# One spectral-mixing kernel: weight runs of 16 KB with real and imaginary rows interleaved on the partitions, pinned TensorE slots from mode 10 on, and filler matmuls behind modes 44 to 59

## The chip, the cores and the metric

The kernel runs on one core of one Trainium2 chip. The metric is the device time of a run in microseconds (us). Repeated runs are given as a median with the lowest and highest. A ratio below is the mean time of one kernel's fast runs over the mean time of the other's fast runs of the same rounds, so it is not quite the ratio of the medians quoted beside it; it comes with a 95% interval, and a difference under 2% counts as "same".

## The reference, cut to what matters

```python
def _attn_ref(q, k, v):                       # all (8, 8, 576, 64) f32
    phi = lambda x: np.where(x > 0, x, np.exp(x) - 1.0) + 1.0
    q_p, k_p = phi(q), phi(k)
    kv = np.einsum('bhsd,bhse->bhde', k_p, v)
    z = np.sum(k_p, axis=2)
    num = np.einsum('bhsd,bhde->bhse', q_p, kv)
    den = np.einsum('bhsd,bhd->bhs', q_p, z)[..., None] + 1e-06
    return num / den

def _moe_ref(x, w_r, w_i, w_ch):              # x (8, 576, 512); w_r, w_i (64, 512, 512) f32
    X = np.fft.rfft(x, axis=1)                # 64 modes are kept
    Yr = np.einsum('bmd,mde->bme', Xr, w_r) - np.einsum('bmd,mde->bme', Xi, w_i)
    Yi = np.einsum('bmd,mde->bme', Xr, w_i) + np.einsum('bmd,mde->bme', Xi, w_r)
    ...
    y = np.fft.irfft(Y, n=S, axis=1)
    u = x + y
    return u + np.maximum(u @ w_ch, 0.0)
```

The two weight tensors are 2 x 64 x 512 x 512 x 4 B = 134 MB of f32. They are read once, and the transfer casts them to bf16 on the way into on-chip memory (SBUF). Each of the 64 modes needs 2.097 MB of f32, its wr and its wi.

Of the kernel before, what the change touches and what calls it, by code (L numbers as in the profile page):

```python
# [42 lines left out]
def kernel(  # L43
# [18 lines left out]
    XDC = 3 * B * NM  # L62
    XTW = NDC * XDC + 2 * B * NM
# [21 lines left out]

    xt_c = xpool.tile([128, XTW], BF16, name="xt_c")
    nc.vector.memset(xt_c[:, NDC * XDC : XTW], 0.0)
    xt_v = xt_c[:, 0 : NDC * XDC].rearrange("p (c t b m) -> p c t b m", c=NDC, t=3, b=B)

    def xt_cols(dc: int, t: int, kk: int):  # L90

        c0 = dc * XDC + t * B * NM + kk
        return xt_c[:, c0 : c0 + 31 * NM + 1 : NM]
# [3 lines left out]
    q_tile = lambda name: xpool.tile([128, QW], F16, tag="qTE", bufs=B + 1, name=name)  # L97
# [3 lines left out]
    W_KEEP = 8  # L101

    def w_load(kk: int, half: int, pool, tag: str, bufs: int):
        name, src = (("wr", moe_w_r), ("wi", moe_w_i))[half]
        w = pool.tile([128, NDC, D], BF16, tag=tag, bufs=bufs, name=f"{name}{kk}")
        rows_of = src[kk].rearrange("(p dc) e -> p dc e", dc=NDC)
        for dcs in (slice(0, 3), slice(3, 4)) if (kk, half) == (NM - 1, 1) else (slice(0, NDC),):
            tc.keep_in_program_order(nc.gpsimd.dma_start(out=w[:, dcs], in_=rows_of[:, dcs, :]))  # L108
        return w

    w_in: dict[int, list] = {}


    W_PRE = 12
# [4 lines left out]
    n_pre, n_keep = W_PRE // 2, W_KEEP // 2  # L119
# [7 lines left out]
    def w_next():  # L127
        kk, half = pending.pop(0)
        pool, tag, bufs = (wpool, "w", W_KEEP) if kk < n_keep else (wpre, "wp", W_PRE)
        w_in.setdefault(kk, []).append(w_load(kk, half, pool, tag, bufs))  # L130
# [153 lines left out]

    def transform(b, dc):
# [17 lines left out]
        if dc == NDC - 1:  # L303
            pin(nc.vector.tensor_copy(out=xt_v[:, :, 1:3, b, :], in_=xf))
            pin(nc.scalar.mul(out=xt_v[:, :, 0, b, :], in_=xf[:, :, 1, :], mul=-1.0))
# [7 lines left out]
    for b in range(B):  # L313
# [12 lines left out]
        for jj in range(NJJ + 1):  # L326
            form_x(b, jj)
            if b > 0 and jj in (2, 3):
                transform(b - 1, jj - 2)
# [3 lines left out]
    for dc in range(NDC):  # L333
        transform(B - 1, dc)


    def w_get(kk: int):
        if kk not in w_in:
            w_in[kk] = [w_load(kk, half, wpool, "w", W_KEEP) for half in range(2)]
# [7 lines left out]
    FILL = {61: (2, 2, 1), 62: (5, 3, 3), 63: (6,)}  # L347

    def mode_product(kk: int, ps, stage, yt_ps):

        wr, wi = w_get(kk)
        st = stage.tile([128, D], F16, tag="ystage", bufs=2, name=f"ys{kk}")
        fixed = pin if kk >= NF else (lambda ins: ins)
        fill = FILL.get(kk, (0, 0, 0))
        P = ps.tile([128, D], F32, tag="P", bufs=2, name=f"P{kk}")
        for t, w in ((1, wr), (0, wi)):
            for dc in range(NDC):
                fixed(
                    nc.tensor.matmul(  # L359
                        P[dc * 32 : dc * 32 + 32, :], xt_cols(dc, t, kk), w[:, dc, :],  # L360
                        start=(t == 1), stop=(t == 0), tile_position=(0, dc * 32),
                    )
                )
            if t == 1:
                work_slot(kk, 0)
                keep_warm(fill[0])
        if kk % 2 == 0:
            fixed(nc.vector.tensor_copy(out=st, in_=P))  # L368
        else:
            fixed(nc.scalar.copy(out=st, in_=P))  # L370
        work_slot(kk, 1)
        keep_warm(fill[1])
# [6 lines left out]
        keep_warm(fill[2])  # L379

    work: list = []
# [7 lines left out]
    def last_mode(ps):  # L389

        kk = NM - 1
        wr, wi = w_get(kk)
        y_last = ps.tile([128, NDC, 2 * B], F32, tag="P", bufs=2, name="y_last")

        def product(t, w, dcs):
            for dc in dcs:
                c0 = dc * XDC + t * B * NM + kk
                x = xt_c[:, c0 : c0 + (2 * B - 1) * NM + 1 : NM]
                for ec in range(NDC):
                    pin(  # L400
                        nc.tensor.matmul(
# [473 lines left out]
```

## The kernel before: the parts that the change touches

The kernel first forms the attention for 8 batches and their spectra `xt_c`. Then it goes through 64 modes. A mode multiplies the spectra by wr and wi (tile `P`, "the P matmuls"), copies `P` out and turns it (`yt`). Other TensorE work is put between: attention rows in modes 10 to 31 (`nw`), inverse transforms and channel products in modes 32 to 55, and the rows of the last modes (`z`, `yp`, `yb`, `zb`) in modes 56 to 60. After the last mode come a tail of matmuls, adds and the stores.

```python
    xt_c = xpool.tile([128, XTW], BF16, name="xt_c")   # per column: -imag, real, imag
    W_KEEP = 8                                         # 8 half-mode tiles = 4 modes

    def w_load(kk, half, pool, tag, bufs):             # 128 partitions, one 8 KB f32 run each
        name, src = (("wr", moe_w_r), ("wi", moe_w_i))[half]
        w = pool.tile([128, NDC, D], BF16, tag=tag, bufs=bufs, name=f"{name}{kk}")
        rows_of = src[kk].rearrange("(p dc) e -> p dc e", dc=NDC)          # NDC = 4
        for dcs in (slice(0, 3), slice(3, 4)) if (kk, half) == (NM - 1, 1) else (slice(0, NDC),):
            tc.keep_in_program_order(nc.gpsimd.dma_start(out=w[:, dcs], in_=rows_of[:, dcs, :]))
        return w
    # ... cut
    FILL = {61: (2, 2, 1), 62: (5, 3, 3), 63: (6,)}    # filler matmuls

    def mode_product(kk, ps, stage, yt_ps):
        wr, wi = w_get(kk)
        fixed = pin if kk >= NF else (lambda ins: ins) # NF = 32: earlier modes are left to the scheduler
        P = ps.tile([128, D], F32, tag="P", bufs=2, name=f"P{kk}")
        for t, w in ((1, wr), (0, wi)):                # 4 matmuls with wr, then 4 with wi
            for dc in range(NDC):
                fixed(nc.tensor.matmul(
                    P[dc * 32 : dc * 32 + 32, :], xt_cols(dc, t, kk), w[:, dc, :],
                    start=(t == 1), stop=(t == 0), tile_position=(0, dc * 32)))
            if t == 1:
                work_slot(kk, 0)                       # other TensorE work between wr and wi
                keep_warm(fill[0])
        # ... cut: copy P out
        work_slot(kk, 1)
        # ... cut: yt
    # ... cut
    QUADS = (5, 6)                                     # batches stored in one piece of four tiles
    for kk in range(n_early, NM):                      # n_early = 10
        mode(kk)
        if kk < NF:                                    # attention rows, left to the scheduler
            for i in spread(len(tiles), kk - n_early, NF - n_early):
                attention_rows(tiles[i])
```

## Time and profile before

| | before |
|---|---|
| time, first 3 runs | 427.85 us (427.78 to 427.94) |
| span of the profiled run | 425.4 us |
| last weight lands, tail after it | 393.03 us, 32.4 us |
| one mode in the weight stream | 4.916 us |
| DMA share and landed rate, 160 to 180 us | 1.06, 213 GB/s |

The first lines are from the page of before, the part that cuts the span into 40 slices. Each digit of PEclk is the TensorE clock that was granted, in tenths of full speed; each digit of DMA is the busy share of the 16 transfer engines in tenths, 9 being 90% or more. GB/s is what landed, so bf16 for the weights.

```profile
PEclk9999866565555855555555587989999899999998
DMA  9999999999999999999999999999999999998797
GB/s 215 208 208 209 209 210 209 212 212 215 218 211 214 214 212 215 214 213 214 212 214 213 213 214 213 214 214 213 213 213 214 214 213 213 213 213 157 250 394 295
DMA packets 35502, 93.12 MB, mean 219 GB/s; under 512 B 3024, under 2 KB 15696, under 8 KB 35216
```

The DMA row has no gap until slice 36 (383 to 393 us), and the rate is flat. Nearly all packets land in less than 8 KB: one weight packet is 4 KB of bf16.

The second view is the chain of waits of before in order of time: start, length, and what was waited for.

```profile
156.94 18.65 DMA wi<-in_moe_w_i_dram
...
176.60 18.65 DMA wi<-in_moe_w_i_dram
...
196.26 18.65 DMA wi<-in_moe_w_i_dram
...
215.92 18.65 DMA wi<-in_moe_w_i_dram
...
235.59 18.64 DMA wi<-in_moe_w_i_dram
...
378.55 14.44 DMA wi<-in_moe_w_i_dram
393.03 0.30 PE y_last L401 x4
```

Each step of 19.66 us is four modes: a load is issued when the tile of four modes earlier comes free. So a mode takes (235.59 - 156.94) / 16 = 4.916 us. The last line is the first work that the last weight allowed.

The third view is the windows of before: a stretch, its length, the busy time of each engine with its instructions, the granted clock, the DMA share and the landed GB/s.

```profile
core 0: us, PE busy (x) PEld busy (x) DVE busy (x) ACT busy (x) POOL busy (x), PEclk, DMA share, GB/s
12.00:16.00 4.00, 1.11 (x22) 1.22 (x24) 2.80 (x4) 0.62 (x1) 1.30 (x2) 1.00 1.21 207
...
160.00:180.00 20.00, 12.11 (x142) 7.24 (x142) 10.84 (x37) 1.17 (x2) 4.23 (x8) 0.50 1.06 213
...
400.00:405.00 5.00, 5.00 (x34) 1.53 (x32) 4.87 (x5) 4.28 (x8) 0.00 (x0) 1.00 0.99 394
```

The first row is q, k and v, in runs of 2,304 B; the second is weights alone; the third is the store. In all three the transfers are full, so the kernel is bound by them nearly from end to end.

### The profile page before, as it was taken

What the parts mean: (1) busy time and instruction counts of PE and PEld (TensorE: products, weight loads), DVE (VectorE), ACT (ScalarE), POOL (GpSimd) and SP (SyncE); (2) the same over time, 40 slices, a digit from 0 to 9 for tenths busy, and PEclk for the clock granted to TensorE, in tenths of its full rate; (3) what the DMA queues carried; (4) which work ended last, traced back from release to release, by engine and by line L of the source; (5) the groups of instructions that cost most, each with busy time, mean ns of one, the idle gap of its engine ahead of it and who ended that gap; (6) DMA issues with size and microseconds to landing.
All of it is one profiled execution on the core that took longest, in us unless ns stands there. A gap on an engine that the chain in (4) does not pass through costs nothing.

```text
span 425.4 us, 6619 instructions
## 1 busy us (share of the span) xinstructions
PE 285.7 (67%) x2692; PEld 160.0 (38%) x2692; DVE 214.5 (50%) x440; ACT 154.1 (36%) x241; POOL 88.3 (21%) x159
## 2 busy tenths in 40 slices
PE   1358777887119765666333689778677778998992
PEld 0246555674003433333111334434334334473420
DVE  4598999956002755556200433433444244421793
ACT  4677776630102100000000244434443354430781
POOL 4222223222201322122112122112122121110000
PEclk9999866565555855555555587989999899999998
DMA  9999999999999999999999999999999999998797
GB/s 215 208 208 209 209 210 209 212 212 215 218 211 214 214 212 215 214 213 214 212 214 213 213 214 213 214 214 213 213 213 214 214 213 213 213 213 157 250 394 295
DMA packets 35502, 93.12 MB, mean 219 GB/s; under 512 B 3024, under 2 KB 15696, under 8 KB 35216
## 3 DMA queue, kind: packets, MB, share of 16 engines
q0 software_dynamic: 31360, 81.48, 98.3%
q1 hardware_dynamic: 4112, 11.22, 7.1%
q8 instruction: 21, 0.34, 0.3%
q14 instruction: 9, 0.07, 0.0%
HBM read 163.93 MB, written 9.44 MB: 407 GB/s over the span
## 4 chain that ended last, share of the span: by engine, by line
DMA 69%; PE 12%; issue 8%; DVE 7%; ACT 2%; POOL 1%; DVEq 0%; POOLq 0%; ACTq 0%
DMA wi<-in_moe_w_i_dram 51%; DMA wr<-in_moe_w_r_dram 9%; DMA k<-in_k_dram 9%; PE acc L641 3%; PE P L359 2%; DVE x L277 2%; PE acc L680 2%; ACT ke L190 1%; PE z L604 1%; DVE ke L203 1%; DVE k L197 1%; PE zb L631 1%; PE zb L630 1%; DVE qe L203 1%; PE yb L626 1%
## 5 line engine op out<-in xcount | busy, mean ns | idle before, releaser
L359 PE MATMUL P<-wi,xt_c 128*32 128x512 bf16 x252 | 37.9, 536 | 38.7 <-DMA wi<-in_moe_w_i_dram 38.6
L370 ACT CAST ys<-P 128x512 f16<-128x512 f32 x31 | 18.2, 586 | 121.6 <-PE P L359 106.8
L108 POOL DMA_DIRECT2D wr<-in_moe_w_r_dram x64 | 34.1, 533 | 130.6 <-PE P L359 91.0
L368 DVE CAST ys<-P 128x512 f16<-128x512 f32 x32 | 22.1, 691 | 72.0 <-PE P L359 49.8
L108 POOL DMA_DIRECT2D wi<-in_moe_w_i_dram x65 | 34.6, 532 | 111.8 <-PE P L359 88.2
L359 PEld LDWEIGHTS <-xt_c 128*32 128x32 bf16 x504 | 28.7, 156 | 75.8 <-issue 64.4
L359 PE MATMUL P<-wr,xt_c 128*32 128x512 bf16 x252 | 37.6, 550 | 24.6 <-DMA wr<-in_moe_w_r_dram 22.5
L563 DVE TENSOR_TENSOR x_main<-ya,x_main 128x512 f32<-128x512 f32 x32 | 22.1, 691 | 43.7 <-PE ya L559 43.6
L582 PE MATMUL eps<-wch,xTw 128*128 128x512 f16 x144 | 41.2, 414 | 0.0
L144 PEld LDWEIGHTS <-qT 64*128 64x128 f16 (+1 forms) x640 | 25.3, 126 | 41.6 <-issue 21.3
L565 ACT CAST x16w<-x_main 128x512 f16<-128x512 f32 x32 | 19.8, 618 | 37.4 <-DVE x_main L563 37.4
L375 PE MATMUL yt<-pick_sb,ys 128*128 128x16 f16 x252 | 16.6, 176 | 24.1 <-DMA pick_sb<-row_pick 15.2
L590 ACT CAST E<-eps 128x512 f16<-128x512 f32 (+1 forms) x40 | 21.3, 543 | 25.5 <-PE eps L582 25.5
L144 PE MATMUL num<-kv,qT 64*128 64x65 f16 (+1 forms) x320 | 13.8, 227 | 20.7 <-ACT kv L250 18.0
L375 PEld LDWEIGHTS <-ys 128*128 128x128 f16 x252 | 12.3, 103 | 39.8 <-issue 16.6
L190 ACT ACTIVATE qe<-q 128x1152 f16<-128x1152 f16 (+1 forms) x16 | 17.8, 1157 | 17.8 <-DMA q<-in_q_dram 17.8
L219 PE MATMUL qTp<-id,qe 128*128 128x128 f16 x144 | 16.7, 309 | 10.1 <-DVE qe L203 9.5
L144 PE MATMUL nw<-kv,qT 64*128 64x65 f16 (+1 forms) x320 | 22.1, 236 | 1.6 <-DVE x_tail L533 1.0
L277 DVE TENSOR_TENSOR x<-num,rd 128x512 f16<-128x512 f32 x32 | 22.1, 692 | 1.1
L190 ACT ACTIVATE ke<-k 128x1152 f16<-128x1152 f16 x16 | 17.7, 1155 | 6.6 <-DMA k<-in_k_dram 6.0
L690 ACT ACTIVATE acc<-acc 128x512 f32<-128x512 f32 x34 | 18.1, 581 | 2.3 <-PE acc L641 1.3
L219 PEld LDWEIGHTS <-qe 128*128 128x128 f16 x144 | 14.5, 146 | 11.2 <-DVE qe L203 9.9
(104 smaller groups left out, 442.5 us busy)
## 6 DMA issues: line engine op xcount, KB each, us to landing
wr<-in_moe_w_r_dram POOLq DMA_DIRECT2D x64, 512.0 KB, 18.6
wi<-in_moe_w_i_dram POOLq DMA_DIRECT2D x63, 512.0 KB, 18.7
k<-in_k_dram POOLq DMA_DIRECT2D x8, 576.0 KB, 14.5
v<-in_v_dram POOLq DMA_DIRECT2D x8, 576.0 KB, 16.6
out_dram<-x_main SPq DMA_DIRECT2D x9, 512.0 KB, 3.1
q<-in_q_dram POOLq DMA_DIRECT2D x7, 576.0 KB, 13.8
out_dram<-x_main SPq DMA_DIRECT2D x2, 1024.0 KB, 5.2
out_dram<-x_main SPq DMA_DIRECT2D x6, 256.0 KB, 3.4
```

The lines of the kernel that those rows point to most:

```text
L108: tc.keep_in_program_order(nc.gpsimd.dma_start(out=w[:, dcs], in_=rows_of[:, dcs, :]))
L144: mm = nc.tensor.matmul(num[hpo][orow, c0 : c0 + 65], qT[rows, hpp, h2, cols], kv_sb[rows, hpp, h2, :])
L190: pin(nc.scalar.activation(out=ev[:, c], in_=heads(nm, b, c), func=AF.Exp))
L219: nc.tensor.transpose(qT_ps[:, j].rearrange("p t r -> p (t r)"), phi["q", b][:, hpp, j].rearrange("p o d -> p (o d)"), id16,)
L277: nc.vector.tensor_tensor(out=dst.rearrange("p (o c d) -> p o c d", o=2, c=4), in0=nv[:, :, :, 0:64], in1=rden.unsqueeze(3).broadcast_to([ ...
L359: nc.tensor.matmul(P[dc * 32 : dc * 32 + 32, :], xt_cols(dc, t, kk), w[:, dc, :], start=(t == 1), stop=(t == 0), tile_position=(0, dc * 32),)
L368: fixed(nc.vector.tensor_copy(out=st, in_=P))
L375: nc.tensor.matmul(yt_ps[:, ec, kk % 8, :], st[:, ec * 128 : ec * 128 + 128], pick_sb)
L563: pin(nc.vector.tensor_tensor(out=x, in0=acc, in1=x, op=ALU.add))
L565: pin(nc.scalar.copy(out=x16w[t], in_=x))
L582: nc.tensor.matmul(e_ps, xT[:, c, :], wch16[:, c, :], start=(c == 0), stop=(c == NDC - 1))
L590: pin(nc.scalar.copy(out=dst, in_=e_ps[:, cols]))
```

## The change

Its intent is a weight stream of longer runs. A half of a mode now goes to 64 partitions with a run of 16 KB each: wr to the even partitions and wi to the odd ones of one tile. The matmul then contracts real and imaginary rows at once, so the spectra must be laid out alike (`place_x`). All 8 matmuls of a mode now need both halves, and both come free together. Around this, TensorE work is pinned from mode 10 on, with all of a mode's other work behind its P matmuls, and three fillers stand behind each of modes 44 to 59. Batch 0 loses eight of its matmuls in modes 56 to 60 (`zb`), which come back as four in mode 61, and batch 5 is stored in pairs of tiles.

```diff
-    W_KEEP = 8
+    W_KEEP = 4
+    PIECES = (slice(0, 4), slice(4, 6), slice(6, 7), slice(7, 8))
     def w_load(kk, half, pool, tag, bufs):
-        name, src = (("wr", moe_w_r), ("wi", moe_w_i))[half]
-        w = pool.tile([128, NDC, D], BF16, tag=tag, bufs=bufs, name=f"{name}{kk}")
-        rows_of = src[kk].rearrange("(p dc) e -> p dc e", dc=NDC)
+        if half == 0:
+            w_in[kk] = pool.tile([128, NDW, D], BF16, tag=tag, bufs=bufs, name=f"w{kk}")   # NDW = 8
+        rows_of = (moe_w_r, moe_w_i)[half][kk].rearrange("(p dc) e -> p dc e", dc=NDW)
+        for dcs in PIECES if (kk, half) == (NM - 1, 1) else (slice(0, NDW),):
+            ... nc.gpsimd.dma_start(out=w_in[kk][half::2, dcs], in_=rows_of[:, dcs, :])
...
+    place = sA.tile([128, 2, 2, 128], BF16, name="place")      # rows of the identity, spread by two
+                pin(nc.vector.tensor_copy(out=place[:, i, o, o::2], in_=id16[:, i::2]))
+    def place_x(b):                                            # per batch, moves rows to even and odd partitions
+        for i in range(2):
+            for o, ts in ((0, slice(1, 3)), (1, slice(0, 2))):
+                pin(nc.tensor.matmul(ps[:, i], place[:, i, o, :],
+                    x[:, ts].rearrange("p t c m -> p (t c m)"), start=(o == 0), stop=(o == 1)))
+        ...                                                    # then one DVE and one ACT copy into xt_c
...
-    FILL = {61: (2, 2, 1), 62: (5, 3, 3), 63: (6,)}
+    FILL = {**{kk: (0, 3) for kk in range(44, 60)}, 60: (0, 1), 61: (2, 3), 62: (4, 6)}
...
-        fixed = pin if kk >= NF else (lambda ins: ins)
+        fixed = pin if kk >= n_early else (lambda ins: ins)
+        for dc in range(NDW):
+            c = dc % NDC * 32
+            n = 32 if dc < NDC else 2 * B
+            fixed(nc.tensor.matmul(P[c : c + n, :], xt_cols(dc, kk, n), w[:, dc, :],
+                start=(dc < NDC), stop=(dc >= NDC), tile_position=(0, c), skip_group_check=True))
...
+        work_slot(kk, 0)
         work_slot(kk, 1)
...
-    QUADS = (5, 6)
+    QUADS = (6,)
...
+    work[:0] = [lambda t=t: attention_rows(t) for t in tiles]  # attention rows pinned into the slots
...
     for kk in range(n_early, NM):
         mode(kk)
-        if kk < NF:
-            for i in spread(len(tiles), kk - n_early, NF - n_early):
-                attention_rows(tiles[i])
```

More of the change, by code (lines that the diff above doesn't have):

```diff
@@ L61 @@
     NJJ = 4
-    XDC = 3 * B * NM
-    XTW = NDC * XDC + 2 * B * NM
+    NDW = 2 * NDC
+    XDC = 2 * B * NM
     NL = 8
@@ L84, with xt_cols @@
     nc.scalar.activation(out=actwarm, in_=actwarm, func=AF.Exp)
-    xt_c = xpool.tile([128, XTW], BF16, name="xt_c")
-    nc.vector.memset(xt_c[:, NDC * XDC : XTW], 0.0)
-    xt_v = xt_c[:, 0 : NDC * XDC].rearrange("p (c t b m) -> p c t b m", c=NDC, t=3, b=B)
-    def xt_cols(dc: int, t: int, kk: int):
-        c0 = dc * XDC + t * B * NM + kk
-        return xt_c[:, c0 : c0 + 31 * NM + 1 : NM]
+    xt_c = xpool.tile([128, NDW * XDC], BF16, name="xt_c")
+    xt_v = xt_c.rearrange("p (c t b m) -> p c t b m", c=NDW, t=2, b=B)
+    def xt_cols(dc: int, kk: int, n: int):
+        c0 = dc * XDC + kk
+        return xt_c[:, c0 : c0 + (n - 1) * NM + 1 : NM]
     QW = 4 * NJ * NP
-    q_tile = lambda name: xpool.tile([128, QW], F16, tag="qTE", bufs=B + 1, name=name)
+    q_tile = lambda name: xpool.tile([128, QW], F16, tag="qTE", bufs=B, name=name)
     kv_all = [xpool.tile([128, 2, 2, 65], F16, tag="kv", bufs=B, name=f"kv{b}") for b in range(B)]
     rd_all = [xpool.tile([128, 5, 2, 4], F32, tag="rd", bufs=B, name=f"rd{b}") for b in range(B)]
-    W_KEEP = 8
+    W_KEEP = 4
+    PIECES = (slice(0, 4), slice(4, 6), slice(6, 7), slice(7, 8))
     def w_load(kk: int, half: int, pool, tag: str, bufs: int):
-        name, src = (("wr", moe_w_r), ("wi", moe_w_i))[half]
-        w = pool.tile([128, NDC, D], BF16, tag=tag, bufs=bufs, name=f"{name}{kk}")
-        rows_of = src[kk].rearrange("(p dc) e -> p dc e", dc=NDC)
-        for dcs in (slice(0, 3), slice(3, 4)) if (kk, half) == (NM - 1, 1) else (slice(0, NDC),):
-            tc.keep_in_program_order(nc.gpsimd.dma_start(out=w[:, dcs], in_=rows_of[:, dcs, :]))
-        return w
-    w_in: dict[int, list] = {}
-    W_PRE = 12
+        if half == 0:
+            w_in[kk] = pool.tile([128, NDW, D], BF16, tag=tag, bufs=bufs, name=f"w{kk}")
+        rows_of = (moe_w_r, moe_w_i)[half][kk].rearrange("(p dc) e -> p dc e", dc=NDW)
+        for dcs in PIECES if (kk, half) == (NM - 1, 1) else (slice(0, NDW),):
+            tc.keep_in_program_order(
+                nc.gpsimd.dma_start(out=w_in[kk][half::2, dcs], in_=rows_of[:, dcs, :])
+            )
+    w_in: dict[int, object] = {}
+    W_PRE = 6
     wpre_ctx, sA_ctx, psA_ctx = ExitStack(), ExitStack(), ExitStack()
@@ L118 @@
     psA = psA_ctx.enter_context(tc.tile_pool(name="psA", bufs=1, space=bass.MemoryType.PSUM))
-    n_pre, n_keep = W_PRE // 2, W_KEEP // 2
+    n_pre, n_keep = W_PRE, W_KEEP
     pin = tc.keep_in_program_order
@@ L129, in w_next @@
         pool, tag, bufs = (wpool, "w", W_KEEP) if kk < n_keep else (wpre, "wp", W_PRE)
-        w_in.setdefault(kk, []).append(w_load(kk, half, pool, tag, bufs))
+        w_load(kk, half, pool, tag, bufs)
     def rows_of(jj: int, base: int = 0):
@@ L283, in form_x, with make_place @@
         )
+    place = sA.tile([128, 2, 2, 128], BF16, name="place")
+    nc.vector.memset(place, 0.0)
+    def make_place():
+        for i in range(2):
+            for o in range(2):
+                pin(nc.vector.tensor_copy(out=place[:, i, o, o::2], in_=id16[:, i::2]))
+    xsp = {}
+    def place_x(b):
+        x = xsp.pop(b)
+        ps = psA.tile([128, 2, 512], F32, tag="big", bufs=3, name=f"xp{b}")
+        for i in range(2):
+            for o, ts in ((0, slice(1, 3)), (1, slice(0, 2))):
+                pin(
+                    nc.tensor.matmul(
+                        ps[:, i], place[:, i, o, :], x[:, ts].rearrange("p t c m -> p (t c m)"),
+                        start=(o == 0), stop=(o == 1),
+                    )
+                )
+        pin(
+            nc.vector.tensor_copy(
+                out=xt_v[:, 0:NDC, :, b, :],
+                in_=ps[:, 0].rearrange("p (t c m) -> p c t m", t=2, c=NDC),
+            )
+        )
+        pin(
+            nc.scalar.copy(
+                out=xt_v[:, NDC:NDW, :, b, :],
+                in_=ps[:, 1].rearrange("p (t c m) -> p c t m", t=2, c=NDC),
+            )
+        )
     def transform(b, dc):
@@ L303, in transform @@
         if dc == NDC - 1:
-            pin(nc.vector.tensor_copy(out=xt_v[:, :, 1:3, b, :], in_=xf))
-            pin(nc.scalar.mul(out=xt_v[:, :, 0, b, :], in_=xf[:, :, 1, :], mul=-1.0))
+            xsp[b] = sA.tile([128, 3, NDC, NM], BF16, tag="xsp", bufs=2, name=f"xsp{b}")
+            xv = xsp[b].rearrange("p t c m -> p c t m")
+            pin(nc.scalar.copy(out=xv[:, :, 1:3, :], in_=xf))
+            pin(nc.scalar.mul(out=xv[:, :, 0, :], in_=xf[:, :, 1, :], mul=-1.0))
     load(0)
@@ L327 @@
             form_x(b, jj)
+            if b == 0 and jj == 0:
+                make_place()
+            if b > 1 and jj == 1:
+                place_x(b - 2)
             if b > 0 and jj in (2, 3):
@@ L332 @@
             transform(b - 1, 3)
-    for dc in range(NDC):
-        transform(B - 1, dc)
+    transform(B - 1, 0)
+    transform(B - 1, 1)
+    place_x(B - 2)
+    transform(B - 1, 2)
+    transform(B - 1, 3)
+    place_x(B - 1)
     def w_get(kk: int):
         if kk not in w_in:
-            w_in[kk] = [w_load(kk, half, wpool, "w", W_KEEP) for half in range(2)]
+            for half in range(2):
+                w_load(kk, half, wpool, "w", W_KEEP)
         return w_in.pop(kk)
@@ L345, in keep_warm @@
             pin(nc.tensor.matmul(last_ps[0], id16, wch16[:, 0, :]))
-    FILL = {61: (2, 2, 1), 62: (5, 3, 3), 63: (6,)}
+    FILL = {**{kk: (0, 3) for kk in range(44, 60)}, 60: (0, 1), 61: (2, 3), 62: (4, 6)}
+    work: list = []
     def mode_product(kk: int, ps, stage, yt_ps):
-        wr, wi = w_get(kk)
+        w = w_get(kk)
         st = stage.tile([128, D], F16, tag="ystage", bufs=2, name=f"ys{kk}")
-        fixed = pin if kk >= NF else (lambda ins: ins)
-        fill = FILL.get(kk, (0, 0, 0))
+        fixed = pin if kk >= n_early else (lambda ins: ins)
+        fill = FILL.get(kk, (0, 0))
         P = ps.tile([128, D], F32, tag="P", bufs=2, name=f"P{kk}")
-        for t, w in ((1, wr), (0, wi)):
-            for dc in range(NDC):
-                fixed(
-                    nc.tensor.matmul(
-                        P[dc * 32 : dc * 32 + 32, :], xt_cols(dc, t, kk), w[:, dc, :],
-                        start=(t == 1), stop=(t == 0), tile_position=(0, dc * 32),
-                    )
-                )
-            if t == 1:
-                work_slot(kk, 0)
-                keep_warm(fill[0])
+        for dc in range(NDW):
+            c = dc % NDC * 32
+            n = 32 if dc < NDC else 2 * B
+            fixed(
+                nc.tensor.matmul(
+                    P[c : c + n, :], xt_cols(dc, kk, n), w[:, dc, :],
+                    start=(dc < NDC), stop=(dc >= NDC), tile_position=(0, c), skip_group_check=True,
+                )
+            )
         if kk % 2 == 0:
@@ L370, in mode_product @@
             fixed(nc.scalar.copy(out=st, in_=P))
+        work_slot(kk, 0)
         work_slot(kk, 1)
-        keep_warm(fill[1])
+        keep_warm(fill[0])
         for ec in range(NDC):
@@ L378, in mode_product @@
             )
-        keep_warm(fill[2])
-    work: list = []
+        keep_warm(fill[1])
     per_slot: dict[int, list] = {}
@@ L391, in last_mode @@
         kk = NM - 1
-        wr, wi = w_get(kk)
+        w = w_get(kk)
         y_last = ps.tile([128, NDC, 2 * B], F32, tag="P", bufs=2, name="y_last")
-        def product(t, w, dcs):
-            for dc in dcs:
-                c0 = dc * XDC + t * B * NM + kk
-                x = xt_c[:, c0 : c0 + (2 * B - 1) * NM + 1 : NM]
-                for ec in range(NDC):
-                    pin(
-                        nc.tensor.matmul(
-                            y_last[:, ec, :], w[:, dc, ec * 128 : ec * 128 + 128], x,
-                            start=(t == 1 and dc == 0 and ec == 0), stop=(t == 0 and dc == NDC - 1),
-                            skip_group_check=True,
-                        )
-                    )
-        product(1, wr, range(NDC))
-        keep_warm(FILL[kk][0])
-        product(0, wi, range(3))
-        product(0, wi, range(3, NDC))
+        for dc in range(NDW):
+            for ec in range(NDC):
+                pin(
+                    nc.tensor.matmul(
+                        y_last[:, ec, :], w[:, dc, ec * 128 : ec * 128 + 128], xt_cols(dc, kk, 2 * B),
+                        start=(dc == 0 and ec == 0), stop=(dc == NDW - 1), skip_group_check=True,
+                    )
+                )
         nc.vector.tensor_copy(out=Y8[:, :, NL - 1, :], in_=y_last)
@@ L467, in mode @@
             if kk < NF:
-                nc.vector.tensor_copy(out=YE_T[:, :, kk - 7 : kk + 1, :], in_=yt_ps)
+                ins = nc.vector.tensor_copy(out=YE_T[:, :, kk - 7 : kk + 1, :], in_=yt_ps)
+                if kk >= n_early:
+                    pin(ins)
             else:
@@ L526, in attention_rows @@
         for b, jj, orow in parts_of(t):
-            nv = num_matmuls(num, orow, q_view(qT_all[b]), kv_all[b], rows_of(jj, BASE[b % 2]))
+            nv = num_matmuls(num, orow, q_view(qT_all[b]), kv_all[b], rows_of(jj, BASE[b % 2]), True)
             for o in range(2):
@@ L531, in attention_rows @@
                     rden = sW.tile([128, 4], F32, tag="rdw", bufs=4, name=f"rdw{t}_{o}")[orow]
-                    nc.vector.reciprocal(out=rden, in_=nv[o][:, :, 64])
-                nc.vector.tensor_tensor(
-                    out=x[orow, o * 256 : o * 256 + 256].rearrange("p (c d) -> p c d", c=4),
-                    in0=nv[o][:, :, 0:64],
-                    in1=rden.unsqueeze(2).broadcast_to([orow.stop - orow.start, 4, Dh]),
-                    op=ALU.mult,
+                    pin(nc.vector.reciprocal(out=rden, in_=nv[o][:, :, 64]))
+                pin(
+                    nc.vector.tensor_tensor(
+                        out=x[orow, o * 256 : o * 256 + 256].rearrange("p (c d) -> p c d", c=4),
+                        in0=nv[o][:, :, 0:64],
+                        in1=rden.unsqueeze(2).broadcast_to([orow.stop - orow.start, 4, Dh]),
+                        op=ALU.mult,
+                    )
                 )
@@ L627, in fold_lead @@
         pin(nc.vector.tensor_tensor(out=x, in0=acc, in1=x, op=ALU.add))
+        if b == 0:
+            return
         e = E0[b][:, jj * D : jj * D + D]
@@ L758, with first_rows @@
         per_slot[kk] = [len(spread(n_form, 2 * (kk - NE) + s, 10)) for s in range(2)]
+    def first_rows(n: int):
+        for i, t in enumerate(pairs[n]):
+            on_bank(
+                n, {i},
+                nc.tensor.matmul(
+                    accs[n][:, i], inv2_sb[0 : 2 * NF, rows_of(t, BASE[0])], YZ[0][0 : 2 * NF, 1, :],
+                    start=False, stop=False, skip_group_check=True,
+                ),
+            )
+    work[:0] = [lambda t=t: attention_rows(t) for t in tiles]
+    for kk in range(n_early, NF):
+        per_slot[kk] = [
+            len(spread(len(tiles), 2 * (kk - n_early) + s, 2 * (NF - n_early))) for s in range(2)
+        ]
     for kk in range(n_early, NM):
         mode(kk)
-        if kk < NF:
-            for i in spread(len(tiles), kk - n_early, NF - n_early):
-                attention_rows(tiles[i])
         if kk == NE + 4:
@@ L770 @@
             )
-            per_slot[NE + 5] = [1, 1]
+            per_slot[NE + 5] = [2, 2]
             for n in range(N_PRE):
-                work.append(lambda n=n: channels(n))
+                work += [lambda n=n: channels(n), lambda n=n: first_rows(n)]
     z1_ps = psW.tile([128, NDC, 8, 2 * B], F32, tag="yt", bufs=1, name="z1l")
```

## The prediction

> # Prediction
>
> **What bounds the kernel now.** Transfers, until the last weight. In the slices of the span the DMA row reads 9 (90% or more) up to 393 us; the windows view gives DMA share 1.06 and 213 GB/s landed (bf16; 426 GB/s of f32 read) from 100 to 388 us. The chain of waits is 69% DMA; from mode 20 to 48 it repeats every 19.66 us for four modes: 4.916 us per 2.097 MB mode. The last weight lands at 393.03 us; of the 32.4 us of tail about 27 are the 9.44 MB store (DMA share 0.96 to 1.03 from 400 to 420 us).
>
> **What the change does, costed.**
>
> 1. Weight runs. A weight DMA has 128 runs of 8 KB in f32; after, 64 of 16 KB: 4 instead of 8 data packets per engine. At 4.916 us a mode an engine's 8 KB take 307.2 ns. The Trainium skill, "DMA: Bandwidth & Descriptors" (Specifications; Why small descriptors are slow), states a ceiling of 435 GB/s, 301.2 ns for 8 KB, and about 3 cycles per packet. The trace agrees: its q/k/v stretch (12 to 34 us, 2,304-byte runs) lands 207 GB/s, 89.0 ns a run, 4.3 ns over the ceiling; weights are 6.0 over. A cost f per packet and c per DMA on each engine (32f+c=137, 8f+c=48) gives f=3.7, c=18 ns. Four packets fewer save 15 ns per DMA, x128 = **1.9 us** (estimate); at most 3.1 us.
>    Even and odd partitions, instead of two halves, keep each transfer on all 16 ports by the map in "SBUF — State Buffer" (Door 1): no loss expected; this trace cannot show it.
> 2. Buffers. Four modes fit as before, but both halves come free only after all 8 matmuls. POOL's gap of 9.7 us between issues (to 140.4 us) did not lower the DMA share. **0**.
> 3. Placing x: per batch 4 matmuls 128x512, one more ACT copy (about 0.6 us), DVE unchanged. In the DVE-bound attention stage (18 to 19.4 of 20 us) DMA stays full and ten prefetched modes hide a few us: **0**.
> 4. Pinning from mode 10; fillers behind 44 to 59 (3 x about 0.22 us a mode); batch 0 without zb (8 matmuls, 4 ACT copies). PE is busy 14.4 to 17.4 of 20 us from 240 to 360 us, 100% from 370 to 384 (modes 57 to 60). Fillers add about what zb takes away; weights are released before a slot's work. The clock is 1.00 from 340 us but for one dip. **0 to -0.7 us** at the stream's end.
> 5. Tail: batch 5 stores in pairs, not a quad; store-bound: **0** (±0.5).
>
> **Prediction: 425.4 us**, 8 in 10 within 421.8 to 428.6. Chances: over 2% faster 0.06, within 2% 0.90, over 2% slower 0.04.
>
> **What would show it.** 1: pitch 4.87-4.89 us a mode, 214 to 215 GB/s in the windows, landed packets of 8 KB instead of 4. 2: DMA share above 1 from 100 to 385 us. 3: first P matmul a few us later, no dip in DMA. 4: clock near 1.00 from mode 44, without the total following. 5: last landing (near 390.8 us) to end stays 31.5 to 33 us.
>
> **What would make it wrong.** Long packets split at the old size (gain 0); ports contended, since each engine now writes two ports (slower by per cents); PE behind in modes 56 to 60; or the whole distance to the ceiling recovered (6 us).

## The result, and the profile after

| | before | after |
|---|---|---|
| time, 6 runs each | 427.81 us (427.13 to 427.94) | 425.74 us (424.89 to 426.46) |
| ratio | | 0.9955 (0.9937 to 0.9973) |
| span of the profiled run | 425.4 us | 423.1 us |
| last weight lands | 393.03 us | 391.17 us |
| tail after it | 32.4 us | 31.9 us |
| one mode in the weight stream | 4.916 us | 4.890 us |

The page of after, the same lines of the slices:

```profile
PEclk9999788889755555555555578989999999999997
DMA  9999999999999999999999999999999999998697
GB/s 215 207 208 209 209 209 210 216 213 215 219 212 215 218 212 215 217 212 215 217 213 214 217 214 214 216 215 214 214 216 215 215 214 215 215 215 162 239 401 304
DMA packets 27550, 93.12 MB, mean 220 GB/s; under 512 B 3072, under 2 KB 15744, under 8 KB 19264
```

There are 7,952 packets fewer, and 8,286 instead of 286 are of 8 KB or more: the long runs did become long packets. The rate rises by about 1 GB/s.

The chain of waits of after, in order of time:

```profile
142.60 17.60 DMA w<-in_moe_w_i_dram
...
160.25 1.13 PE P L409 x5
...
162.18 17.56 DMA w<-in_moe_w_i_dram
...
179.78 1.14 PE P L409 x7
...
199.35 1.13 PE P L409 x6
...
218.90 1.14 PE P L409 x6
...
238.49 1.13 PE P L409 x8
...
374.47 15.34 DMA w<-in_moe_w_i_dram
389.85 1.29 PE y_last L444 x28
391.17 0.30 PE y_last L444 x4
```

The chain still goes through the weights (the DMA lines; the others of its kind are left out). A P group starts when its wi has landed, so a mode takes (238.49 - 160.25) / 16 = 4.890 us. The last four products wait for the last piece, at 391.17 us.

The windows of after:

```profile
core 0: us, PE busy (x) PEld busy (x) DVE busy (x) ACT busy (x) POOL busy (x), PEclk, DMA share, GB/s
12.00:16.00 4.00, 1.08 (x22) 1.17 (x24) 2.84 (x4) 0.61 (x1) 1.26 (x2) 1.00 1.21 208
...
160.00:180.00 20.00, 8.30 (x116) 4.03 (x120) 8.06 (x24) 1.17 (x2) 4.24 (x8) 0.50 1.03 215
...
400.00:405.00 5.00, 5.00 (x32) 1.40 (x30) 4.92 (x6) 4.44 (x10) 0.00 (x0) 1.00 1.01 404
```

The q, k, v stretch and the store keep their full share. The weight stretch lands 215 instead of 213 GB/s, at a DMA share of 1.03 instead of 1.06. So 1.86 of the 2.3 us between the two profiled runs lie before the last weight, and 0.4 us behind it.

### The profile page after: what moved, and what is told of

It is laid out like the page before. It is cut to its first block, busy times and chain, and to the rows that moved or that the text cites. A ratio compares the mean times of both kernels' runs of the same rounds, so it can differ in the third digit from the quotient of the medians.

```text
span 423.1 us, 6734 instructions
## 1 busy us (share of the span) xinstructions
PE 274.3 (65%) x2755; PEld 142.8 (34%) x2762; DVE 216.1 (51%) x444; ACT 159.1 (38%) x253; POOL 89.3 (21%) x161
## 4 chain that ended last, share of the span: by engine, by line
DMA 70%; PE 15%; ACT 4%; DVE 4%; issue 3%; POOL 3%; DVEq 0%; ACTq 0%; POOLq 0%
DMA w<-in_moe_w_i_dram 59%; DMA k<-in_k_dram 7%; PE P L409 5%; DMA pick_sb<-row_pick 4%; PE acc L684 3%; PE acc L723 2%; POOL w L109 2%; ACT ke L191 2%; ACT qT L227 1%; PE yt L423 1%; DVE x L278 1%; ACT qe L191 1%; DVE ys L415 0%; ACT ys L417 0%; POOL k L173 0%
## 5 line engine op out<-in xcount | busy, mean ns | idle before, releaser
L409 PE MATMUL P<-w,xt_c 128*32 128x512 bf16 (+1 forms) x504 | 58.1, 537 | 78.8 <-DMA w<-in_moe_w_i_dram 74.9
L109 POOL DMA_DIRECT2D w<-in_moe_w_r_dram x64 | 33.7, 526 | 215.9 <-PE P L409 193.2
L409 PEld LDWEIGHTS <-xt_c 128*32 128x32 bf16 (+1 forms) x504 | 16.0, 158 | 89.2 <-DMA w<-in_moe_w_i_dram 64.3
L109 POOL DMA_DIRECT2D w<-in_moe_w_i_dram x67 | 36.2, 541 | 22.7 <-DMA w<-in_moe_w_i_dram 16.3
L623 PE MATMUL eps<-wch,xTw 128*128 128x512 f16 x144 | 39.8, 403 | 0.0
L145 PEld LDWEIGHTS <-qT 64*128 64x128 f16 (+1 forms) x640 | 20.9, 125 | 51.8 <-issue 39.2
L573 DVE TENSOR_TENSOR x_main<-nw,rd 128x256 f32<-128x256 f32 x32 | 11.5, 415 | 13.9 <-PE nw L145 13.9
L227 ACT COPY qT<-qTp 128x1152 f16<-128x1152 f16 x16 | 17.1, 1124 | 0.7 <-PE qTp L220 0.2
```

Source lines behind the costliest of these rows:

```text
L109: nc.gpsimd.dma_start(out=w_in[kk][half::2, dcs], in_=rows_of[:, dcs, :])
L145: mm = nc.tensor.matmul(num[hpo][orow, c0 : c0 + 65], qT[rows, hpp, h2, cols], kv_sb[rows, hpp, h2, :])
L227: nc.scalar.copy(out=qT[:, hpp].rearrange("p t (r j) -> p t r j", j=NJ), in_=qT_ps.rearrange("p j t r -> p t r j"),)
L409: nc.tensor.matmul(P[c : c + n, :], xt_cols(dc, kk, n), w[:, dc, :], start=(dc < NDC), stop=(dc >= NDC), tile_position=(0, c), skip_group_ ...
L623: nc.tensor.matmul(e_ps, xT[:, c, :], wch16[:, c, :], start=(c == 0), stop=(c == NDC - 1))
```

## The experiments

Twelve experiments ran, two of them the changed kernel itself, four on each of three chips. Times are medians of all runs; only pairs had slow ones (two of six). Executions over 1.5% slower than the fastest of the same kernel are left out of the means. The column "last weight" is when the last four products of the last mode began; in the rows marked PE, TensorE did not wait there, so the time tells when TensorE got to the last mode (the start of its last products), not when the weight landed. The kernel before has 427.4 to 427.7 us on all three (medians of 9 to 11 runs).

| kernel | runs | time, us | ratio to before | last weight, us |
|---|---|---|---|---|
| after_again | 5 | 426.29 (425.03 to 426.31) | 0.9966 (0.9952 to 0.9979) | 391.28 |
| runs_8k | 5 | 426.84 (426.72 to 426.89) | 0.9985 (0.9971 to 0.9999) | 392.98 |
| runs_8k_two_dmas | 4 | 430.56 (429.45 to 431.20) | 1.0069 (1.0053 to 1.0085) | 395.52 |
| runs_4k_wrong | 4 | 430.99 (430.39 to 431.64) | 1.0082 (1.0066 to 1.0098) | 396.70 |
| halves | 4 | 425.62 (425.08 to 426.41) | 0.9960 (0.9947 to 0.9972) | 392.38 |
| pairs | 6 | 437.14 (433.29 to 441.67) | 1.0198 (1.0170 to 1.0226) | 405.67, PE |
| unpinned | 6 | 428.78 (426.78 to 429.66) | 1.0020 (0.9999 to 1.0041) | 395.16, PE |
| no_fill | 4 | 427.25 (426.30 to 428.00) | 0.9995 (0.9981 to 1.0009) | 393.60, PE |
| before_order | 5 | 427.36 (427.19 to 427.94) | 0.9994 (0.9982 to 1.0006) | 393.81, PE |
| unpinned_no_fill | 4 | 427.72 (426.93 to 430.40) | 1.0016 (0.9989 to 1.0044) | first product 391.03 |
| quads56 | 5 | 425.21 (425.15 to 426.48) | 0.9946 (0.9935 to 0.9958) | 391.40 |
| after_third | 6 | 425.68 (424.99 to 426.42) | 0.9951 (0.9938 to 0.9964) | 391.30 |

All results were right except that of runs_4k_wrong.

### The changed kernel twice more

No edit.

> The changed kernel once more, unchanged, beside the variants of this call. Its six earlier times fall in two groups, 424.9 to 425.2 and 426.3 to 426.5 us. All theories: median 424.9 to 426.5 us, ratio to before 0.993 to 0.997, pitch of the weight stream 4.888 us a mode. If the two groups come from the chip and not from the run, all times of this call lie in one group; if from the run, both groups show again.

> The changed kernel on the same chip and in the same rounds as the three others, as their reference: 424.9 to 426.5 us, ratio 0.994 to 0.998. If its profiled run is of the upper group (above 426 us), the trace should show a last weight about 1.1 us later, as the profiled run of halves did, with the clock still 1.00 in modes 56 to 60; a lower clock there would show that the two groups come from TensorE instead.

All 17 runs of the changed kernel fall in two groups: 424.9 to 425.2 us (7 runs) and 426.2 to 426.5 us (10 runs). Both groups occur on the same chip within minutes, so the chip doesn't make them. All three profiled runs are of the lower group, with the last weight at 391.17, 391.28 and 391.30 us, so no trace of an upper run of this kernel exists. The profiled run of halves (426.05 us) is at that height: its last weight came at 392.38 us, and its granted clock was 1.00 from 355 to 395 us. That points to the stream and not to TensorE, but in another kernel and in one run. Its lag comes early: one issue of a load (at 73.44 us) took 1.52 us where the changed kernel's took 0.54, and the next issues came 1.0 to 1.1 us later than in the changed kernel up to 101 us. From 80 to 380 us its landed bytes stay 0.2 to 0.4 us behind (sums of windows of 5 us), and this lag does not grow, so its stream is not slower. What makes the last weight 1.2 us late from there, and what makes the groups, stays open. For the sizes below I use the last weights of profiled runs; means of all runs are given beside them.

### Run length: runs_8k

The rows of a mode are dealt out differently: a partition gets two blocks of four rows, 256 rows apart, so each source run is 8 KB again. Number of DMAs, partitions and the order of work stay as in the changed kernel, and the placing of x follows.

```diff
-        rows_of = (moe_w_r, moe_w_i)[half][kk].rearrange("(p dc) e -> p dc e", dc=NDW)
-            ... dma_start(out=w_in[kk][half::2, dcs], in_=rows_of[:, dcs, :])
+        rows_of = (moe_w_r, moe_w_i)[half][kk].rearrange("(a p dc) e -> p a dc e", a=2, dc=NDC)
+        wv = w_in[kk].rearrange("p (a dc) e -> p a dc e", a=2)
+            ... dma_start(out=wv[half::2], in_=rows_of)
-    ... tensor_copy(out=place[:, i, o, o::2], in_=id16[:, i::2])
+    ... tensor_copy(out=place[:, i, o, o::2], in_=id16[:, i * 64 : i * 64 + 64])
```

> The changed kernel with two source runs of 8 KB a partition in place of one of 16 KB; same partitions, same number of DMAs, same order of work on every engine, right result. Theory (packets): the gain is the packets saved, f = 3.7 ns each per engine, so all of it goes: pitch 4.916 us a mode, landed packets of 4 KB again, time 1.9 us above the changed kernel of this call, ratio to before about 1.000. Rival (order): the gain comes from pinned slots, the earlier release of weights and the finer last pieces: pitch stays 4.888, time within 0.5 us of the changed kernel.

The chain of waits of runs_8k in order of time:

```profile
162.80 17.60 DMA w<-in_moe_w_i_dram
...
182.46 17.61 DMA w<-in_moe_w_i_dram
...
202.12 17.61 DMA w<-in_moe_w_i_dram
...
241.44 17.59 DMA w<-in_moe_w_i_dram
...
392.98 0.30 PE y_last L450 x4
```

and its packets, from the slices of its page:

```profile
DMA packets 35679, 93.12 MB, mean 219 GB/s; under 512 B 3073, under 2 KB 15745, under 8 KB 35521
```

The packets are short again, and a mode takes (241.44 - 162.80) / 16 = 4.915 us, as before the change. The last weight comes 1.73 us later than in the changed kernel (392.98 against 391.25, the mean of its three profiled runs). So 1.73 of the expected 1.9 us came back in the stream. In the times it is 1.8 us against the lower group and 0.8 us against the mean of all five runs of after_again (426.82 against 426.03), because runs_8k has no second group. And runs_8k did not fall back to the kernel before: with the same last weight (392.98 against 393.03) its mean is 0.7 us below (426.82 against 427.53 in the same rounds). About 0.5 us of this lies in the tail (424.9 - 392.98 = 31.9 us against 32.4 before), so that part does not come from the run length.

### Packets and DMAs apart: runs_8k_two_dmas and runs_4k_wrong

The first sends each half of a mode of runs_8k in two DMAs; the second has four runs of 4 KB a partition.

```diff
 # runs_8k_two_dmas, against runs_8k
-            ... dma_start(out=wv[half::2], in_=rows_of)
+            for a in range(2):
+                ... dma_start(out=wv[half::2, a], in_=rows_of[:, a])
 # runs_4k_wrong, against the changed kernel (x is not re-placed: wrong result)
+        rows_of = ....rearrange("(a p dc) e -> p a dc e", a=4, dc=2)
```

> As runs_8k, but each half of a mode comes in two DMAs of 64 runs of 8 KB: packets as in runs_8k, twice the DMAs. Theory with a cost c = 18 ns per DMA on each engine: per mode 4 x (4f + c) = 132 ns over the ceiling against 66 in the changed kernel and 96 in runs_8k, so pitch 4.952 us, time about 4.2 us above the changed kernel. Rival (all cost is per packet, f = 6, c = 0): pitch as in runs_8k (4.916), time about 3.1 us above. Waits on landings 8 DMAs back may halve what is in flight; if that starves the stream, the DMA share falls below 1 in some windows and the time rises more, but the pitch elsewhere still tells.

> The changed kernel with four source runs of 4 KB a partition (the rows then do not match x: the result is wrong on purpose; all work is the same). Theory (f = 3.7, c = 18): 16f + c = 77 ns per DMA over the ceiling against 33: pitch 4.978 us a mode, time about 5.7 us above the changed kernel. Rival (f = 6, c = 0): 96 against 24, pitch 5.01, about 9 us above. Rival (order): no difference beyond 0.5 us.

The pitch of runs_8k_two_dmas was 4.956 us a mode (ten modes from 160.39 to 209.95 us in its chain) where 4.952 was expected, and its last weight was 2.54 us later than in runs_8k. The last weight of runs_4k_wrong was 3.72 us later than in runs_8k and 5.45 us later than in the changed kernel, where 5.7 us was expected. Each of the 16 engines got 127 more DMAs in the first, and 8 more packets in each of 127 DMAs in the second (the last half mode keeps its four pieces). So

- a DMA costs 2.54 us / 127 = 20 ns on each engine (18 estimated from the trace of before),
- a packet costs 3.72 us / 1,016 = 3.7 ns on each engine, and from runs_8k 1.73 us / 508 = 3.4 ns (3.7 estimated).

The pitch of runs_4k_wrong was (241.46 - 161.62) / 16 = 4.990 us in its chain, where 4.978 was expected. Taken from the pitch over such 16 modes, which is a shorter stretch than up to the last weight, a packet costs 3.1 ns (runs_8k) or 4.7 ns (runs_4k_wrong).

The rival that put everything on packets (c = 0) falls: it has no room for the slower runs_8k_two_dmas, which has as many data packets as runs_8k. The page "DMA: Bandwidth & Descriptors" of the Trainium skill (Why small descriptors are slow) gives about 3 cycles of overhead per packet; at the 850 MHz that the page states for the fabric this is an estimate of 3.5 ns, and the measured 3.4 to 3.7 ns agrees with it.

### Even and odd against halves

```diff
-            ... dma_start(out=w_in[kk][half::2, dcs], ...)
+            ... dma_start(out=w_in[kk][HALVES[half], dcs], ...)      # 0 to 63, 64 to 127
-    ... tensor_copy(out=place[:, i, o, o::2], ...)
+    ... tensor_copy(out=place[:, i, o, HALVES[o]], ...)
```

> The changed kernel with the real part on partitions 0 to 63 and the imaginary part on 64 to 127, instead of even and odd; 16 KB runs, all else the same, right result. Theory (ports, the skill's page SBUF): each transfer then reaches 8 of 16 ports, ceiling about 218 GB/s landed against 214.5 that the stream needs, so the stream slows by some per cent where bursts collide: 1 to 4% longer, 430 to 442 us. Rival (ports don't matter, as landed bytes are half of the read ones): within 1 us of the changed kernel.

The rival holds: 425.62 us and 0.9960, within the changed kernel's range. From 160 to 180 us it landed 215 GB/s, as the changed kernel did. By the port map of "SBUF — State Buffer" (Door 1) one such transfer reaches 8 of 16 ports, for which the page states 218 GB/s as the asymptote and 196 measured at 1 MiB. What lands here is bf16, half of what is read, and just fits below the asymptote; also, neighbouring transfers in the queue write opposite halves. The run does not tell these two apart. It does show that the interleave is not what makes the stream fast.

### Half the weight DMAs: pairs

One DMA brings wr (or wi) of two modes, to save the cost per DMA. The buffers stay at four modes in two tiles.

```diff
-    W_KEEP = 4
+    W_KEEP = 2
-            w_in[kk] = pool.tile([128, NDW, D], ...)
+            w_in[kk] = pool.tile([128, 2, NDW, D], ...)
+            ... dma_start(out=w_in[kk][half::2], in_=src[kk : kk + 2].rearrange("m (p dc) e -> p m dc e", ...))
```

> The changed kernel with one DMA for wr (or wi) of two modes: 64 partitions with two runs of 16 KB, so the same packets and half the weight DMAs (66 less). Buffers hold four modes as before but come free by twos. From runs_8k_two_dmas against runs_8k (128 more DMAs, stream ended 2.4 us later on the mean engine) the cost is 18.6 ns per DMA on each engine; theory with c = 18.6 ns: last weight 1.2 us earlier, time 1.2 us below the changed kernel (424.9 to 426.5), so 423.8 to 425.3. Rival (coarse release starves the stream, or PE falls behind by getting two modes at once): no gain or a loss of some us, with the DMA share below 1 somewhere between 130 and 385 us.

It lost: the four fast runs (433.29 to 437.22 us, mean 435.87) lie 8.5 us above the kernel before (ratio 1.0198, "unclear" at the 2% limit) and about 10 us above the changed kernel. The profiled run (440.01 us) is slow. In it the DMA share falls to 0.94 from 290 to 295 us and to 0.73 from 375 to 380 us, as the rival expected: a tile that comes free by two modes leaves only two modes in flight. No fast run was profiled, so for these the reason is not shown. The 1.2 us of the DMA cost were not to be had this way.

### The order of work: unpinned

Modes 10 to 31 and their attention rows are left to the scheduler, as they were before the change. That does not bring the old order back: the scheduler lays the rows out anew for the changed kernel.

```diff
-        fixed = pin if kk >= n_early else (lambda ins: ins)
+        fixed = pin if kk >= NF else (lambda ins: ins)
-    work[:0] = [lambda t=t: attention_rows(t) for t in tiles]
+        if kk < NF:
+            for i in spread(len(tiles), kk - n_early, NF - n_early):
+                attention_rows(tiles[i])
 # and the pins within attention_rows and of the copy to YE_T are taken out
```

> The changed kernel with modes 10 to 31 and their attention rows left to the scheduler again, as before the change; 16 KB runs and fillers stay. My step 4: worth 0, as PE has slack from 140 to 240 us and the stream stays full: within 0.5 us of the changed kernel. Rival (order): the part of the gain that runs_8k did not take back (0.7 us of means) comes from the pinning: about 0.7 us slower.

My expectation was wrong, and the rival's 0.7 us was too small: 428.78 us, mean 428.46, which is 2.4 to 2.8 us above the changed kernel's means on the two other chips (426.03 and 425.69; on this chip halves had 425.68). The windows of unpinned:

```profile
165.00:170.00 5.00, 4.10 (x52) 2.53 (x51) 4.08 (x14) 0.58 (x1) 1.06 (x2) 0.50 1.01 198
170.00:175.00 5.00, 3.96 (x42) 1.56 (x40) 4.29 (x17) 0.00 (x0) 1.06 (x2) 0.50 0.83 156
175.00:180.00 5.00, 2.71 (x28) 0.90 (x28) 1.08 (x2) 1.17 (x2) 2.12 (x5) 0.50 0.96 195
```

and the same stretch in the windows of after:

```profile
165.00:170.00 5.00, 1.95 (x28) 0.88 (x28) 1.42 (x4) 0.59 (x1) 1.06 (x2) 0.50 1.05 218
170.00:175.00 5.00, 2.35 (x32) 1.28 (x36) 2.48 (x7) 0.00 (x0) 1.06 (x2) 0.50 1.05 218
175.00:180.00 5.00, 2.06 (x32) 0.99 (x35) 2.14 (x8) 0.59 (x1) 1.06 (x2) 0.50 1.01 210
```

The transfers run dry. The rate falls to 198, 156 and 195 GB/s; against 216 GB/s that is (18 + 60 + 21) x 5 / 216 = 2.3 us of stream. The reason is in the timeline of the issues (engine POOL) of unpinned: in brackets is how long POOL waited and for whom.

```profile
160.62 0.52 POOL L109 DMA_DIRECT2D w<-in_moe_w_r_dram  x1 [5.21 <-PE nw L145]
...
166.37 0.52 POOL L109 DMA_DIRECT2D w<-in_moe_w_r_dram  x1 [4.69 <-PE nw L145]
...
173.20 0.52 POOL L109 DMA_DIRECT2D w<-in_moe_w_r_dram  x1 [5.78 <-PE P L409]
```

Loads were issued 5.75 and 6.83 us apart, and from 142.16 to 173.20 us 6.2 us apart on the mean of five modes, where the stream uses up a mode in 4.89 us. The scheduler had put more than 40 attention matmuls (`nw`) ahead of a mode's P matmuls, and these alone free a tile, now both halves at once. The kernel before was left to the scheduler too, but there the rows lay further apart. The windows of tile `nw` (TensorE busy and its matmuls, VectorE busy), of before and then of unpinned:

```profile
160.00:170.00 10.00, 2.93 (x43) 5.03 (x21) 0.50 1.05 212
...
160.00:170.00 10.00, 6.62 (x83) 7.71 (x30) 0.50 1.03 206
```

In the timeline of TensorE, 44 to 57 of these matmuls stand between the P matmuls of one mode and the next in unpinned (140 to 172 us), 17 to 33 in before (148 to 179 us), where they also stand between the two halves of a mode. So what starved the stream is this crowding of rows. How much of it the release of both halves at once adds is not shown: no run has the long runs with halves freed apart. From mode 26 to mode 36 every issue is 1.8 to 1.9 us later than in the changed kernel: the stream did not make the loss good. The profiled run lost about 2 us more at the end, at a lower clock: 0.50 from 370 to 375 us (see no_fill), which may be why this kernel's runs spread from 426.78 to 429.66 us (one run was profiled).

### The fillers: no_fill

```diff
-    FILL = {**{kk: (0, 3) for kk in range(44, 60)}, 60: (0, 1), 61: (2, 3), 62: (4, 6)}
+    FILL = {60: (0, 1), 61: (2, 3), 62: (4, 6)}
```

> The changed kernel without the fillers behind modes 44 to 59. My step 4: 0; granted clock dips from 260 to 360 us come back (0.6 to 0.9 in some windows), PE is busier for the same work there, the stream keeps its pitch, time within 0.5 us of the changed kernel. Rival (clock): PE gets behind in modes 56 to 60, last weights are issued later, 0.5 to 2 us slower.

The rival was nearer: 427.25 us, by means 1.2 to 1.5 us above the changed kernel (427.20; the changed kernel had 426.03 and 425.69 on two other chips). The windows of no_fill:

```profile
365.00:370.00 5.00, 4.47 (x28) 1.52 (x24) 1.46 (x3) 1.17 (x2) 0.08 (x1) 0.50 1.03 215
370.00:375.00 5.00, 5.00 (x13) 1.25 (x14) 2.34 (x4) 1.75 (x3) 0.98 (x2) 0.50 1.03 215
...
390.00:395.00 5.00, 4.68 (x61) 2.45 (x60) 1.54 (x3) 0.00 (x0) 0.00 (x0) 1.00 0.05 7
```

and of after:

```profile
365.00:370.00 5.00, 4.60 (x26) 1.38 (x25) 2.65 (x4) 1.33 (x3) 1.05 (x2) 1.00 1.03 215
370.00:375.00 5.00, 5.00 (x52) 3.39 (x52) 1.12 (x2) 2.43 (x5) 1.05 (x3) 1.00 1.02 211
...
390.00:395.00 5.00, 4.41 (x52) 2.92 (x50) 1.90 (x4) 1.93 (x5) 0.56 (x1) 1.00 0.10 20
```

Both streams keep their rate. But the clock of no_fill was 0.50 from 365 to 375 us, and TensorE, busy 5.00 of 5 us, did 13 matmuls from 370 to 375 us where the changed kernel did 52 (of other sizes, too). A mode's 8 P matmuls took 1.12 us at 368.50 us, against 0.69 us in the changed kernel at 367.24 us. It started on the last mode at 393.43 us, where the changed kernel did at 389.85 us. The weights had landed by then (DMA share 0.05 from 390 to 395 us), and its chain has all 32 last products in one piece, without a wait for a load.

```profile
393.60 0.87 PE y_last L444 x32
```

So in this run TensorE and not the stream ended the mode loop, and the span grew by 3.1 us (426.2 against 423.1). "TensorE: Matmul & The Clock Gate" of the Trainium skill (Part 1) has the clock at half after about 3.4 us without work. This trace does not show that condition: the clock fell in a stretch of lower load (0.66 from 360 to 365 us, TensorE busy 3.66 of 5 us), but from 355 to 365 us its longest wait was 1.34 us, up to 361.73 us. So what made it fall, and that the missing fillers did, is not shown.

How dependable the fillers are stays open. The profiled unpinned run had them and dipped all the same (0.50 from 370 to 375 us); that of unpinned_no_fill lacked them and had 0.88 from 365 to 370 and 1.00 from 370 to 375 us.

### The two halves of the change crossed: before_order and unpinned_no_fill

The first is the kernel before with pinning, slots and fillers, but its own weight layout (and with batch 0's eight `zb` matmuls, which the change takes out of modes 56 to 60); the second is the new layout without pinning and fillers.

```diff
 # before_order, against before
-        fixed = pin if kk >= NF else (lambda ins: ins)
+        fixed = pin if kk >= n_early else (lambda ins: ins)
-    FILL = {61: (2, 2, 1), ...
+    FILL = {**{kk: (0, 0, 3) for kk in range(44, 60)}, 61: (2, 2, 1), ...
+    work[:0] = [lambda t=t: attention_rows(t) for t in tiles]      # with their slots, as in the change
 # unpinned_no_fill: the edits of unpinned and of no_fill together
```

> The kernel before with the other half of the change: TensorE work pinned in slots from mode 10 and three fillers behind modes 44 to 59; weights still in 8 KB runs, wr and wi in tiles of their own, freed after 4 matmuls each. Theory (pinning and fillers only pay back what the coarse release of the new layout costs): its stream already lands without a gap, so last weight at 392.5 to 393.5 us and time within 0.5 us of before (ratio 0.999 to 1.001). Rival (pinning and fillers are gains by themselves, as their removal from the changed kernel cost 2.5 and 1.2 us): 1 to 3 us faster than before, ratio 0.993 to 0.998.

> The changed kernel without pinning and without the fillers of modes 44 to 59: the new layout alone, nearly. Theory: the stream starves by about 2 us between 160 and 180 us as in unpinned, and TensorE falls behind in modes 56 to 60 at half clock as in no_fill; the later stream hides part of the second: 428 to 430 us, above the kernel before (ratio 1.001 to 1.006). Rival (the two losses add up fully): 430 us or more. If it is at or below 426.5, the layout alone makes the gain and the two removals were noise.

| us, median | rows left to the scheduler | pinned, fillers |
|---|---|---|
| 8 KB runs, halves freed apart | before 427.74 | before_order 427.36 (0.9994) |
| 16 KB runs, halves freed together | unpinned_no_fill 427.72 (1.0016) | changed kernel 425.68 (0.9951) |

All are of the same chip and rounds. Neither part gains by itself; together they gain 2 us. The left column is not one order, as the scheduler's differs between the two kernels (see unpinned). before_order met the theory in its time; its last products began a little later than expected (393.81 us), without a wait for a load, as TensorE had been busy 5.00 of 5 us from 370 to 390 us. unpinned_no_fill came out a little lower than expected in its median, with a wide spread, and its interval contains 1. Its slices show the dry stretch again: 190 GB/s in slice 16 (170 to 181 us).

### Stores of batch 5: quads56

```diff
-    QUADS = (6,)
+    QUADS = (5, 6)
```

> The changed kernel with batch 5 stored as one quad again. My step 5: within 0.5 us of the changed kernel of this call; the time from the last weight to the end (31.9 us now, 32.4 before) is 31.4 to 32.4 us. Rival (the tail's 0.5 us comes from the pairs): 0.5 us slower, 32.4 us.

The time is 425.21 us and the tail 423.4 - 391.40 = 32.0 us, as in the changed kernel (31.9). The pairs of batch 5 are worth nothing measurable, and they are not the source of the 0.4 us by which the tail is shorter than before. From the last weight to the last add it is equally long in both profiled runs (25.15 and 25.16 us: 418.18 - 393.03 before, 416.33 - 391.17 after); the difference lies in the stores that drain after it. Its cause stays open.

## Why the prediction was right, point by point

The measured 425.74 us lies 0.3 us from the predicted 425.4 us and within the range.

1. **Weight runs, 1.9 us: right in mechanism, and in size for the profiled runs.** The pitch became 4.890 us (predicted 4.87 to 4.89), the last weight came 1.86 us earlier, at 391.17 us (predicted near 390.8), packets of 8 KB landed, and the windows read 213 to 216 GB/s. runs_8k gave 1.73 us of it back with nothing else altered. The two costs solved from the trace of before, f = 3.7 and c = 18 ns, were measured as 3.4 to 3.7 and 20 ns. But all profiled runs are of the lower group; by the means of all runs, runs_8k gave back only 0.8 us. That the total came within 0.3 us is therefore in part luck: the upper group took about as much from the mean as the shorter tail and the rest, which runs_8k shows without long runs (0.7 us), put back. The remark that the interleave is needed to reach all ports was not borne out: halves was as fast.
2. **Buffers, 0: right for the whole change, wrong as an argument.** I had taken a gap of 9.7 us between issues in the trace of before as a sign that the coarser release costs nothing. One gap after a full queue is covered by what is in flight; a row of issues each 1 to 2 us late is not. With the order that the scheduler chose for the new layout such a row came, and the stream ran dry for about 2 us (unpinned). The zero held because the change also pins the order, which this step did not argue: as a result it was luck.
3. **Placing x, 0: right.** The first P matmul came at 109.8 instead of 103.4 us, and the DMA share did not dip (1.03 and 218 GB/s from 100 to 120 us).
4. **Pinning and fillers, 0 to -0.7 us: right as a difference to before, for a reason that I had not seen.** They gain nothing by themselves (before_order, 0.9994). Within the changed kernel they are worth something: without pinning the stream starves by about 2 us, and the kernel without fillers was 1.2 to 1.5 us slower, in its profiled run because TensorE at half clock ended the mode loop. So "without the total following" did not hold for the clock. The zeros of steps 2 and 4 hide a loss of about 2 us and the pinning that avoids it.
5. **Tail, 0 (±0.5): right.** It measured 31.9 against 32.4 us, and quads56 left it at 32.0.

What the prediction did not foresee is the two groups of run times, 1.3 us apart.

## What to carry to other kernels

When a queue of transfers is full from end to end, its cost per packet and per DMA can be solved from two stretches of one trace with different run lengths, and the gain of longer runs can be estimated from them; here the stream's gain came out within 0.2 us in the profiled runs (1.73 against 1.9 us), and the whole change was worth 0.45% (0.9955). Before making buffers coarser, look at how far apart the releases come and not only at whether they are four modes ahead: in unpinned the order of the consumer's other work let the queue run dry. An order left to a scheduler can change when another part of the kernel changes. A part of a change that is worth nothing alone may be what makes another part pay, so remove parts from the changed kernel and also add them to the old one.

## What the Trainium skill lacked or had wrong

- "DMA: Bandwidth & Descriptors": the page gives the fixed time of a DMA as a latency (about 2 us) and calls the semaphore's write nearly free, but does not say what a whole DMA takes from an engine's time when the queue is full. The runs show 20 ns per DMA on each engine (127 more DMAs, last weight 2.54 us later), beside 3.4 to 3.7 ns per packet.
- "SBUF — State Buffer" (Door 1): the page warns that 64 neighbouring partitions get the bandwidth of 32 (196 GB/s measured at 1 MiB). With transfers of 64 partitions each, to the two halves in turn and casting f32 to bf16, halves landed 215 GB/s, as much as with the interleave over all ports. No page says that a cast to half the size leaves room at the ports.
- "TensorE: Matmul & The Clock Gate" (Part 1): the page has full clock back after about 3.4 us of sustained work. In no_fill the granted clock stayed at 0.50 from 365 to 375 us with TensorE busy 4.47 and 5.00 of 5 us, and read 0.63 in the next 5 us; it had fallen with no wait longer than 1.34 us from 355 to 365 us. The same part does warn that on trn2 the clock has been seen stuck low.
- No page says that equal run times of a kernel on one core can fall in two narrow groups (here 424.9 to 425.2 and 426.2 to 426.5 us) at an undisturbed clock.
